# First batch of a fused attention and two-MLP kernel: kind of tile arithmetic and step counts set tile by tile, low parts on VectorE, the next batch's first loads on SP's queue

## The chip, the cores and the metric

The kernel runs on 1 core of one Trainium2 chip. The metric is the device time of one execution in microseconds; the number compared is a median over several executions. A core has TensorE (PE in the rows; its weight loads are PEld), VectorE (DVE), ScalarE (ACT), GpSimd (POOL) and SyncE (SP), which runs no arithmetic here and only issues transfers. Each engine works through its own instructions in the order in which they stand; between engines semaphores order the work. POOL and ACT can issue transfers too.

## The reference, cut to what matters

```python
def _attn_ref(q, k, v, p):                     # 8 batches, 8 heads, 576 rows, 64 columns; p has 32 rows
    scale = 1.0 / np.sqrt(q.shape[-1])
    def sm_attn(qq, kk, vv):
        s = scale * np.matmul(qq, kk.transpose(0, 1, 3, 2))
        s = s - np.max(s, axis=-1, keepdims=True)
        a = np.exp(s)
        a = a / (np.sum(a, axis=-1, keepdims=True) + 1e-09)
        return np.matmul(a, vv)
    p_packed = sm_attn(p, k, v)
    return sm_attn(q, p_packed, p_packed)
...
    x = attn_out.transpose(0, 2, 1, 3).reshape(4608, 512)
    h = x @ w_in;  g = h - np.tanh(h);  x = g @ w_out            # first MLP: 512 -> 2048 -> 512
    h = x @ w_in2; r = np.maximum(h, 0.0)
    return (s * (r * r) + b) @ w_out2                             # second MLP, same sizes
```

The weights of both MLPs come as 64-bit floats, everything else as 32-bit floats.

## The kernel before

**Precision.** TensorE multiplies in a 32-bit format of its own that holds fewer bits than the inputs. Each operand is therefore split into a high part (a rounded copy) and a low part (what the copy left over), and a product is three passes: high by low, high by high, low by high. `gh` and `gl`, `a2h` and `a2l`, and the two halves of each `wo` and `z` tile are such pairs.

**Converting the first MLP's weights.** `w_in1` is handled as four column chunks `w1[c]`, each in two halves (`w1_steps(c, i)`), and `w_out1` as sixteen row tiles (`wo1_steps(j)`). `to_f32` turns 64-bit words into 32-bit floats with one ACT instruction (the absolute value of the high word, L119) and four DVE instructions (L121, L123, L126, L129). A `wo` tile then gets its high part by an ACT cast (L138) and its low part by a subtraction (L140), which stands on GpSimd for tiles 2 to 11 and on VectorE for the others.

**Work per tile.** Batch 0 is 32 tiles in four parts: two halves of the rows by two halves of the 16 hidden tiles. I number them 0 to 31 in the order in which they run; in the names of the instructions `h_0_1_3` is batch 0, row half 1, hidden tile 3, which is tile 11 of this count. A tile is: `mm1` (six passes into one of two PSUM banks `h`, L464), tanh on ACT, the activation h - tanh(h) and its split, and then, two tiles later, `mm2` (twelve passes into the accumulators `acc`, L504). The activation comes in three kinds. Kind "v": DVE subtracts (L473), ACT rounds `gh`, DVE subtracts again for `gl` (L135). Kind "b": DVE subtracts inside the PSUM bank (L481), ACT reads `gh` from it, TensorE subtracts `gh` from the bank with a matrix `minus` (L487), ACT reads `gl` (L488). Kind "p": TensorE does the first subtraction too (L484). In kinds "b" and "p" the bank becomes free for the tile after next only when `gl` has been read.

**What sets the order.** While the tiles are written out, a generator `fill` is advanced by `next(fill)`; one step is about one instruction of the conversions, of the products `z` (`zp`, made of `w1[c]` and the packed attention, which replace attention and first weight by one matrix per batch) or of the next batch's attention. A second generator `more` converts the second MLP's weights. How many steps stand behind each tile is a table: `SLOTS` and `AFTER` before, per part, with `CATCH_UP` later. `in_turn` runs groups of generators one group after the other and may advance the next group's first step early. `until` forces steps where a tile needs their result. So the numbers decide where each instruction stands on each engine. The loads of batch 1 (`second_loads`: `load_p`, `load_k`, `load_v`, `load_q`) are steps of `fill` too; `load_k` and `load_q` are sixteen transfers each of 32 partitions by 9 by 32 floats.

Of the kernel before, what the change touches and what calls it, by code (L numbers as in the profile page):

```python
# [18 lines left out]
def pack_attention_two_mlps(ctx, tc, q, k, v, p, w_in1, w_out1, w_in2, w_out2, s_in, b_in, out):  # L19
# [16 lines left out]
    C = 9  # L36
# [16 lines left out]
    LAND = 14  # L53
    W_K, W_P, W_PK, W_PV, W_E, W_Q = 5, 1, 5, 1, 7, 5

    AFTER, SLOTS = (6, 5, 4, 1), (5, 3, 4, 1)
    HOW = "p" * 8, "b" * 8, "v" * 8, "v" * 8
    AHEAD, CATCH_UP, FIRST_W = 13, 4, (23, 24, 25, 26, 27, 40, 41, 42, 43, 44)
    EXP_LO, EXP_HI = 2.0 ** -15, 2.0 ** 16 * 1.875
    assert 2 * R == P and NB == 2 * C and 4 * M == P and 2 * D == P and H * D == DM  # L60

# [99 lines left out]
    def load_k(b, g):  # L161
        for hp in range(2):
            h0 = 4 * g + 2 * hp
            t = apool.tile([P, 2, C, 32], F32, tag="kr", name=f"k_{b}_{g}_{hp}", bufs=2)
            rows = k[b, h0:h0 + 2].rearrange("h (r a n) d -> a r h n d", a=2, n=C)
            for a in range(2):
                for u in range(2):
                    p0 = (2 * a + u) * 32
                    for e in range(2):
                        nc.gpsimd.dma_start(out=t[p0:p0 + 32, e], in_=rows[a][:, e, :, u * 32:u * 32 + 32])  # L170
            k_t[b, g, hp] = t

    def load_v(b, g):

        t = apool.tile([P, 4, CT * D], F32, tag="v", name=f"v_{b}_{g}", bufs=1)
        src = v[b, 4 * g:4 * g + 4].rearrange("h (r c) d -> r h (c d)", c=C)
        nc.gpsimd.dma_start(out=t[:R], in_=src[:, :, :CT * D])
        nc.gpsimd.dma_start(out=t[R:, :, :(C - CT) * D], in_=src[:, :, CT * D:])
        v_t[b, g] = t.rearrange("r h (c d) -> r h c d", c=CT)


# [49 lines left out]
    def load_q(b, hf):  # L231
        for g in range(G):
            for hp in range(2):
                h0 = 4 * g + 2 * hp
                t = apool.tile([P, HB // 32, 32], F32, tag="qr", name=f"q_{b}_{hf}_{g}_{hp}", bufs=4)
                for u in range(2):
                    for e in range(2):
                        src = q[b, h0 + e, hf * HB:(hf + 1) * HB, u * 32:u * 32 + 32]
                        p0 = (2 * e + u) * 32
                        nc.gpsimd.dma_start(out=t[p0:p0 + 32], in_=src.rearrange("(n r) d -> r n d", r=32))  # L240
                q_t[b, hf, g, hp] = t

    def bank_a(name):
# [312 lines left out]
    with tc.manual_schedule():  # L556
# [51 lines left out]
        def wo1_steps(j):  # L608
            while j == NF - 1 and ("wo", 13) not in done:
                yield  # L610
            src = stg["wo", j]
            x = words(src)[0].bitcast(F32)
            yield from to_f32(x, src, wopool.tile([P, 2, DM], I32, tag=f"wo{j}", name=f"t_{j}")[:, 0])
            yield from split_wo(j, "wo1", nc.gpsimd if 1 < j < 12 else nc.vector, x)
            done.add(("wo", j))
            if j in (5, 7):
                load_wo1(j + 3, j + 4)
            if j == 11:
                load_wo1(13)
            if j == NF - 1:  # L620
                free()
# [16 lines left out]

        def in_turn(*groups):

            groups = [[call_late(g) for g in group] for group in groups]
            for n, group in enumerate(groups):
                for i, _ in enumerate(both(group)):
                    yield
                    if i == min(AHEAD, 4 * len(group)) and n + 1 < len(groups):
                        for g in groups[n + 1]:
                            next(g)

        def call_late(f):
            g, *a = f  # L650
            yield from g(*a)

        def until(key, gen):
            forced.append(key)
# [16 lines left out]
        take_turn()  # L671
        load_wo1(0, 1, 2, 3, 4, 5, 6, 7)
        make_identity(nc, ident)
        nc.scalar.mul(minus, ident, -1.0)
        nc.vector.memset(ones, 1.0)

        run(step_p(0))
# [13 lines left out]
        def first_weights():  # L691
            yield from in_turn(
                [(w1_steps, 1, 0)], [(w1_steps, 1, 1)],
                [(wo1_steps, 0), (wo1_steps, 1)],
                [(first_z, 1), (wo1_steps, 2), (wo1_steps, 3)],
                [(wo1_steps, 4), (wo1_steps, 5)],
                [(second_stage, 0, 1), (wo1_steps, 6), (wo1_steps, 7)],
                [(w1_steps, 2, 0)], [(w1_steps, 2, 1)],
                [(wo1_steps, 8), (wo1_steps, 9)],
                [(first_z, 2), (wo1_steps, 10), (wo1_steps, 11)],  # L700
                [(w1_steps, 3, 0)], [(w1_steps, 3, 1)],
                [(wo1_steps, 12), (wo1_steps, 13), (second_loads,)],
                [(first_z, 3), (wo1_steps, 14), (wo1_steps, 15)])

        pend = []

# [103 lines left out]
        def slot():  # L810
            ticks[0] += 1
            if owed[0]:
                owed[0] -= 1
                next(fill, None)
            if ("wo", NF - 1) not in done:
                n = SLOTS[part[0]]
                for _ in range(ticks[0] * n // 6 - (ticks[0] - 1) * n // 6):
                    next(fill)
                return
            if ticks[0] % 3 == 1:  # L820
                next(more, None)
            next(fill, None)

        owed = [0]

        def owe():
# [4 lines left out]
        for b in range(B):  # L831
            if b:
                parts = [(hf, range(NF)) for hf in range(2)]
            else:
                parts = [(hf, js) for js in (range(NF // 2), range(NF // 2, NF)) for hf in range(2)]
            for hf, js in parts:
                part[0] += 1
                last = (b == B - 1 and hf == 1)
                if last:
                    until(("a", b, hf), fill)  # L840
                    run(fill)
                    run(more)
                    att.close()
                    second = SecondMLP(tc, ctx, wslot, w2_d, wo2_d, x2t, g2_d, s_sb, bias, out)
                    fill = second.early(lambda c: (B - 1, 1, c) in mm1_done)
                acc = new_acc(f"{b}_{hf}_{js[0]}")
                for j in js:
                    c = j // CH
                    until(("z", b, c), fill)
                    until(("a", b, hf), fill)  # L850
                    h = mm1(b, hf, j, slot)
                    if ("wo", NF - 1) not in done:
                        for _ in range(AFTER[part[0]]):
                            next(fill)
                    elif ("a", 1, 0) not in done:
                        for _ in range(CATCH_UP):
                            next(fill)
                    if j % CH == CH - 1:
                        mm1_done.add((b, hf, c))
                    how = HOW[part[0]][j - js[0]] if b == 0 else "v"  # L860
                    on_pe = how != "v"
                    t = act_bank(h, f"{b}_{hf}_{j}", how == "p") if on_pe else act1(h, f"{b}_{hf}_{j}")
                    if on_pe:
                        next(t)
                    between = None
                    if pend and len(pend[-1]) == 5:
# [471 lines left out]
```

## Time and profile before

| | |
|---|---|
| time, median of 3 executions | 1519.46 us (1517.79 to 1522.28) |
| the profiled execution's own time | 1515.79 us |
| its span, first to last instruction | 1514.0 us |
| TensorE busy over the span | 97% |
| VectorE, ScalarE, GpSimd busy over the span | 71%, 50%, 24% |
| mean granted TensorE clock | 0.990 of full speed |

The profiled execution is one of its own and lies below the three timed ones. Its time is 1.79 us more than its span. Busy shares are averages over the whole kernel; the change touches the first batch, which runs from about 36 to 172 us, and the loads of the second.

### The profile page before, as it was taken

How to read it: one execution, taken by the hardware profiler on the slowest of the kernel's cores; microseconds unless marked ns; L12 is line 12 of the kernel's file. 1: busy time of each engine (PE TensorE's matmuls, PEld its weight loads, DVE VectorE, ACT ScalarE, POOL GpSimd, SP SyncE). 2: the span in 40 equal slices, each digit the busy share in tenths (PEclk: the TensorE clock that was granted, in tenths of full speed). 3: DMA queues.
4: the chain of work that ended last, by engine and by line, in shares of the span. 5: the costliest groups of instructions: out<-in, count | busy, mean ns of one | idle time of the engine just before them, and what ended most of it. 6: DMA issues, size and time to landing. Idle time of an engine off the chain costs nothing.

```text
span 1514.0 us, 28111 instructions
## 1 busy us (share of the span) xinstructions
PE 1463.3 (97%) x10508; PEld 1377.0 (91%) x10508; DVE 1074.3 (71%) x2058; ACT 754.1 (50%) x1459; POOL 357.9 (24%) x576
## 2 busy tenths in 40 slices
PE   6779899999999999999999999999999999999998
PEld 4668798998988889889999999999999999999998
DVE  5886878879687887875555767767777775565564
ACT  4554344444444344443344556656667655454443
POOL 0248452634447274543001000000021000000000
PEclk7899999999999999999999999999999999999999
DMA  9446355544535354332428466465487987676683
GB/s 283 162 135 169 105 147 138 155 132 120 150 98 151 92 141 118 103 94 95 147 100 308 178 229 235 172 260 214 194 296 284 312 258 199 217 239 200 216 248 84
DMA packets 252185, 271.62 MB, mean 179 GB/s; under 512 B 112784, under 2 KB 191888, under 8 KB 252048
## 3 DMA queue, kind: packets, MB, share of 16 engines
q1 hardware_dynamic: 225952, 222.68, 44.9%
q0 software_dynamic: 22368, 46.17, 11.4%
q8 instruction: 82, 1.34, 0.4%
q10 hardware_dynamic: 3728, 0.98, 0.3%
q14 instruction: 55, 0.45, 0.1%
HBM read 161.61 MB, written 108.13 MB: 178 GB/s over the span
## 4 chain that ended last, share of the span: by engine, by line
PE 79%; issue 7%; DVE 6%; DMA 3%; POOL 3%; ACT 2%; SPq 1%; DVEq 0%; POOLq 0%; ACTq 0%
PE acc L504 22%; PE h L464 11%; PE Y L1271 9%; PE Y L1045 8%; PE Z L1271 6%; PE X L1045 6%; PE Z L1045 6%; PE X L1271 6%; PE zp L367 2%; POOL k L170 1%; DMA k<-in_k_dram 1%; DVE gl L135 1%; PE pv L339 1%; SPq L194 1%; DMA g<-g 1%
## 5 line engine op out<-in xcount | busy, mean ns | idle before, releaser
L504 PE MATMUL acc<-gh,wo 128*128 128x288 f32 x2040 | 418.6, 296 | 0.2 <-DVE wo L140 0.2
L504 PEld LDWEIGHTS acc<-gh,wo 128*128 128x128 f32 x2040 | 329.8, 189 | 0.5 <-DVE wo L140 0.4
L504 PE MATMUL acc<-gl,wo 128*128 128x288 f32 x1020 | 309.8, 304 | 5.7 <-ACT wo L138 2.8
L472 ACT ACTIVATE t<-h 128x288 f32<-128x288 f32 x240 | 98.8, 412 | 304.4 <-PE h L464 263.5
L504 PEld LDWEIGHTS acc<-gl,wo 128*128 128x128 f32 x1020 | 192.4, 189 | 34.7 <-issue 20.0
L464 PE MATMUL h<-a2h,z 128*128 128x288 f32 x1024 | 213.9, 297 | 1.5 <-ACT z L445 1.5
L473 DVE TENSOR_TENSOR t<-h,t 128x288 f32<-128x288 f32 x240 | 107.5, 448 | 139.5 <-ACT t L472 138.8
L944 DVE TENSOR_TENSOR x<-B,x 128x768 fp32r<-128x768 f32 x158 | 147.0, 950 | 74.3 <-ACT x L1201 60.4
L464 PE MATMUL h<-a2l,z 128*128 128x288 f32 x512 | 157.9, 308 | 9.8 <-ACT gl L488 6.4
L464 PEld LDWEIGHTS h<-a2h,z 128*128 128x128 f32 x1024 | 165.0, 189 | 2.2 <-ACT z L445 1.7
L240 POOL DMA_DIRECT2D q<-in_q_dram x224 | 135.3, 612 | 130.7 <-DVE qT L374 109.3
L1045 PE MATMUL Y<-x,w 128*128 128x384 f32 x864 | 158.5, 336 | 0.0
L1271 PE MATMUL Y<-x,w 128*128 128x384 f32 x864 | 153.4, 335 | 0.0
L1045 PEld LDWEIGHTS Y<-x,w 128*128 128x128 f32 x864 | 151.3, 188 | 0.0
L1271 PEld LDWEIGHTS Y<-x,w 128*128 128x128 f32 x864 | 150.2, 188 | 0.5 <-ACT x L1201 0.3
L170 POOL DMA_DIRECT2D k<-in_k_dram x224 | 136.6, 617 | 50.2 <-DVE kT L290 40.7
L464 PEld LDWEIGHTS h<-a2l,z 128*128 128x128 f32 x512 | 97.4, 190 | 27.1 <-ACT gl L488 9.4
L1201 ACT CAST x<-B 128x768 fp32r<-128x768 f32 x116 | 93.8, 834 | 42.6 <-DMA B<-g 30.2
L135 DVE TENSOR_TENSOR gl<-t,gh 128x288 fp32r<-128x288 f32 x239 | 110.8, 463 | 0.0
L1045 PE MATMUL X<-x,w 128*128 128x384 f32 x576 | 108.1, 336 | 0.0
L1045 PE MATMUL Z<-x,w 128*128 128x384 f32 x576 | 107.9, 336 | 0.0
L1271 PE MATMUL X<-x,w 128*128 128x384 f32 x576 | 103.0, 336 | 1.5 <-DVE w L944 1.5
(181 smaller groups left out, 2236.4 us busy)
## 6 DMA issues: line engine op xcount, KB each, us to landing
g<-g SPq DMA_DIRECT2D x190, 384.0 KB, 3.3
B<-g SPq DMA_DIRECT2D x116, 384.0 KB, 4.7
w<-w_d POOLq DMA_DIRECT2D x28, 512.0 KB, 6.1
B<-x2t SPq DMA_DIRECT2D x24, 384.0 KB, 5.4
g<-s SPq DMA_DIRECT2D x23, 384.0 KB, 2.8
out_dram<-g SPq DMA_DIRECT2D x184, 48.0 KB, 1.9
x2t<-xs SPq DMA_DIRECT2D x15, 576.0 KB, 3.7
w1s<-in_moe_w_in_dram SPq DMA_DIRECT2D x16, 512.0 KB, 8.1
```

The costliest lines, as they stand in the source:

```text
L135: (eng or nc.vector).tensor_tensor(out=lo, in0=x, in1=hi.bitcast(F32), op=ALU.subtract)
L170: nc.gpsimd.dma_start(out=t[p0:p0 + 32, e], in_=rows[a][:, e, :, u * 32:u * 32 + 32])
L240: nc.gpsimd.dma_start(out=t[p0:p0 + 32], in_=src.rearrange("(n r) d -> r n d", r=32))
L367: nc.tensor.matmul(ps[e][i * M:(i + 1) * M, :rhs(i).shape[-1]], pblk[b][r, h // 4, h % 4 * M:h % 4 * M + M], rhs(i)[r], start=True, stop=True)
L464: nc.tensor.matmul(h[:, :HB], zt[:, zi, g, f0:f0 + P], a[:, g], start=(n == 0), stop=(n == 3 * G - 1))
L472: nc.scalar.activation(t, h[:, :HB], AF.Tanh)
L473: nc.vector.tensor_tensor(out=t, in0=h[:, :HB], in1=t, op=ALU.subtract)
L504: nc.tensor.matmul(acc[m][:, :HB], w[:, m * P:(m + 1) * P], x, start=(j == js[0] and i == 0), stop=(j == js[-1] and i == 2))
L944: self.nc.vector.tensor_tensor(out=o, in0=a, in1=b, op=op)
L1045: self.nc.tensor.matmul(bank[:, f, :self.TH], w[:, f, a, kt], x[:, b, kt], start=(p in ("P1", "P5", "P6") and m == 0), stop=(m == 5), skip ...
L1201: self.nc.scalar.copy(self.xs[(7 * self.NBK + n) % self.XS][:, 0], self.ready[0])
L1271: nc.tensor.matmul(bank[:, ft, :T], w[:, kk, u, ft], x[:, v, kk], start=first and p in ("P1", "P5", "P6"), stop=last, skip_group_check=True)
```

## The change

Seven edits go together.

- The kind of each of batch 0's 32 tiles stands in one string `HOW`, and the number of `fill` steps per tile in one table `STEPS`. Before it was eight "p", eight "b", sixteen "v" (kinds per part). After it is sixteen "p", nine "b", seven "v". A tile's steps are spread over its six slots; the extra steps right behind `mm1` (`AFTER`, `CATCH_UP`) are gone.
- All low parts of `wo` are made by VectorE.
- `in_turn` advances the next group's first step (the absolute value on ACT) once each generator of the present group has run once, and only for weight conversions.
- Batch 1's K, V and Q are loaded by SP's queue instead of GpSimd's, and their step comes before the conversion of `w1[3]`.
- The conversion of `wo` tiles 12 and 13 stands beside `first_z(3)`, 14 and 15 after it.
- `more` starts, as before, when the last `wo` tile is done, but the slots of `fill` go on by the table until batch 1's first attention is done.
- `minus` is made by GpSimd from a zeroed tile instead of by ScalarE.

```diff
-    AFTER, SLOTS = (6, 5, 4, 1), (5, 3, 4, 1)
-    HOW = "p" * 8, "b" * 8, "v" * 8, "v" * 8
-    AHEAD, CATCH_UP, FIRST_W = 13, 4, (23, 24, 25, 26, 27, 40, 41, 42, 43, 44)
+    STEPS = 9, 13, 14, 11, 15, 10, 12, 15, 0, 6, 9, 13, 7, 5, 0, 2, 6, 3, 10, 5, 6, 10, 11, 11, 18, 14, 15, 13, 12, 13, 10, 8
+    HOW = "ppbbpppppppppvvvvvvpppvbbbbpbbbp"
+    FIRST = (0, 0, 8), (1, 0, 8), (0, 8, 16), (1, 8, 16)
...
-                        nc.gpsimd.dma_start(out=t[p0:p0 + 32, e], in_=rows[a][:, e, :, u * 32:u * 32 + 32])
+                        (nc.gpsimd if b > 1 else nc.sync).dma_start(out=t[p0:p0 + 32, e], in_=rows[a][:, e, :, u * 32:u * 32 + 32])
...
-            yield from split_wo(j, "wo1", nc.gpsimd if 1 < j < 12 else nc.vector, x)
+            yield from split_wo(j, "wo1", nc.vector, x)
...
-                    if i == min(AHEAD, 4 * len(group)) and n + 1 < len(groups):
-                        for g in groups[n + 1]:
-                            next(g)
+                    if i == len(group) and n + 1 < len(groups):
+                        for f, g in groups[n + 1]:
+                            if f in (w1_steps, wo1_steps):
+                                next(g)
...
-        nc.scalar.mul(minus, ident, -1.0)
+        nc.vector.memset(csum, 0.0)
+        nc.gpsimd.tensor_tensor(out=minus, in0=csum[:, 0], in1=ident, op=ALU.subtract)
...
+                [(second_loads,)],
                 [(w1_steps, 3, 0)], [(w1_steps, 3, 1)],
-                [(wo1_steps, 12), (wo1_steps, 13), (second_loads,)],
-                [(first_z, 3), (wo1_steps, 14), (wo1_steps, 15)])
+                [(first_z, 3), (wo1_steps, 12), (wo1_steps, 13)],
+                [(wo1_steps, 14), (wo1_steps, 15)])
...
-            if ("wo", NF - 1) not in done:
-                n = SLOTS[part[0]]
-                for _ in range(ticks[0] * n // 6 - (ticks[0] - 1) * n // 6):
+            if ("wo", NF - 1) in done and ticks[0] % 3 == 1:
+                next(more, None)
+            if ("a", 1, 0) in done or tile[0] >= len(STEPS):
+                next(fill, None)
+                return
+            n = STEPS[tile[0]]
+            for _ in range(ticks[0] * n // 6 - (ticks[0] - 1) * n // 6):
+                if ("a", 1, 0) not in done:
                     next(fill)
-                return
-            if ticks[0] % 3 == 1:
-                next(more, None)
-            next(fill, None)
...
-                    if ("wo", NF - 1) not in done:
-                        for _ in range(AFTER[part[0]]):
-                            next(fill)
-                    elif ("a", 1, 0) not in done:
-                        for _ in range(CATCH_UP):
-                            next(fill)
...
-                    how = HOW[part[0]][j - js[0]] if b == 0 else "v"
+                    how = HOW[tile[0]] if b == 0 else "v"
```

SP's order after the first store of partial sums, before the change. `wo1s_13` is the raw form of `wo` tile 13, `wo1s_7` that of tiles 14 and 15 together, `pc_1` batch 1's P, `xs` and `xp` the partial sums.

```order
L522 DMA x2t_138<-xs_0_0_906 512x1x288
L599 DMA wo1s_13_1033<-in_moe_w_out_dram 128x512
L229 DMA pc_1_1085<-in_p_dram 128x2x64 x2
L581 DMA wo1s_7_1088<-in_moe_w_out_dram 128x2x512
L522 DMA x2t_138<-xs_0_1_1273 512x1x288
```

The same place on SP after the change:

```order
L600 DMA wo1s_13_1038<-in_moe_w_out_dram 128x512
L230 DMA pc_1_1059<-in_p_dram 128x2x64 x2
L171 DMA k_1_0_0_1065<-in_k_dram 32x9x32 x8
L171 DMA k_1_0_1_1074<-in_k_dram 32x9x32 x8
L178 DMA v_1_0_1124<-in_v_dram 64x4x320
L179 DMA v_1_0_1124<-in_v_dram 64x4x256
L241 DMA q_1_0_0_0_1136<-in_q_dram 32x9x32 x4
L241 DMA q_1_0_0_1_1141<-in_q_dram 32x9x32 x4
L241 DMA q_1_0_1_0_1146<-in_q_dram 32x9x32 x4
L241 DMA q_1_0_1_1_1151<-in_q_dram 32x9x32 x4
L582 DMA wo1s_7_1228<-in_moe_w_out_dram 128x2x512
```

Thirty-four transfers of batch 1 now stand between the raw `wo` tile 13 and the raw tiles 14 and 15.

VectorE's order around the end of `wo` tiles 10 and 11 and the conversion of `w1[3]`, before the change (`t_10` is scratch; `h_0_1_3` and the like are the first subtraction of a tile of kind "b"):

```order
L481 TENSOR_TENSOR h_0_1_3_964<-h_0_1_3_964,t_0_1_3_976 128x288
L129 SCALAR_TENSOR_TENSOR wo1s_10_761<-wo1s_10_761,t_10_933 128x512
L129 SCALAR_TENSOR_TENSOR wo1s_11_763<-wo1s_11_763,t_11_935 128x512
L481 TENSOR_TENSOR h_0_1_4_998<-h_0_1_4_998,t_0_1_4_1013 128x288
L121 TENSOR_SCALAR w1_3_836<-w1_3_836 128x1024
L123 TENSOR_SCALAR w1_3_836<-w1_3_836 128x1024
L126 SCALAR_TENSOR_TENSOR w1_3_836<-w1s_3_0_837,w1_3_836 128x1024
L129 SCALAR_TENSOR_TENSOR w1_3_836<-w1s_3_0_837,w1_3_836 128x1024
```

The same place after the change:

```order
L141 TENSOR_TENSOR wo1_10_1010<-wo1s_10_758,wo1_10_1010 128x512
L141 TENSOR_TENSOR wo1_11_1012<-wo1s_11_760,wo1_11_1012 128x512
L474 TENSOR_TENSOR t_0_1_5_1043<-h_0_1_5_1034,t_0_1_5_1043 128x288
L474 TENSOR_TENSOR t_0_1_6_1090<-h_0_1_6_1083,t_0_1_6_1090 128x288
L136 TENSOR_TENSOR gl_1_0_1_6_1094<-t_0_1_5_1043,gh_1_0_1_6_1093 128x288
L474 TENSOR_TENSOR t_0_1_7_1116<-h_0_1_7_1109,t_0_1_7_1116 128x288
L136 TENSOR_TENSOR gl_1_0_1_7_1120<-t_0_1_6_1090,gh_1_0_1_7_1119 128x288
L122 TENSOR_SCALAR w1_3_862<-w1_3_862 128x1024
L474 TENSOR_TENSOR t_0_0_8_1171<-h_0_0_8_1163,t_0_0_8_1171 128x288
L136 TENSOR_TENSOR gl_1_0_0_8_1175<-t_0_1_7_1116,gh_1_0_0_8_1174 128x288
```

The two low parts have come onto VectorE, and the conversion of `w1[3]`, which stood behind tile 12's subtraction, now stands behind those of tiles 13 to 15.

ScalarE's order around the absolute value of `wo` tile 14 after the change (`z_0_3` is the product `z` of chunk 3):

```order
L473 ACTIVATE t_0_0_10_1258<-h_0_0_10_1249 128x288
L135 CAST gh_1_0_0_10_1261<-t_0_0_9_1203 128x288
L120 ACTIVATE t_14_1265<-wo1s_7_1228 128x512
L433 CAST z_0_3_1230<-zp_0_3_0_1231 128x512
L433 CAST z_0_3_1230<-zp_0_3_1_1232 128x512
L480 ACTIVATE t_0_0_11_1294<-h_0_0_11_1286 128x288
L135 CAST gh_1_0_0_11_1298<-t_0_0_10_1258 128x288
L139 CAST wo1_12_1308<-cv_139 128x512
L139 CAST wo1_13_1313<-wo1s_13_1038 128x512
L486 CAST gh_0_0_11_1295<-h_0_0_11_1286 128x288
L446 CAST z_0_3_1230<-zp_0_3_0_1231 128x512
L446 CAST z_0_3_1230<-zp_0_3_1_1232 128x512
```

The instruction that needs the raw tile 14 now stands ahead of all four casts of `z_0_3` and of tile 19's tanh; before, it stood after tile 15's tanh, and ahead of the same casts.

## Rows read from the trace of the kernel before

**Rows 1.** Three stretches: length; busy us (instructions) PE, PEld, DVE, ACT, POOL; PEclk; DMA share; GB/s.

```profile
35.70:74.61 38.91, 30.68 (x177) 24.23 (x178) 34.17 (x60) 23.33 (x49) 8.13 (x6) 0.87 0.47 175
74.61:111.38 36.77, 27.27 (x186) 21.82 (x186) 32.71 (x53) 21.04 (x47) 15.95 (x20) 0.95 0.47 141
...
122.77:171.62 48.85, 43.67 (x422) 33.53 (x420) 32.85 (x87) 18.54 (x55) 31.99 (x53) 1.00 0.59 143
```

**Rows 2.** TensorE's timeline: start, length, what, count, [idle before, and what ended it].

```profile
55.12 0.65 PE L484 MATMUL h<-t,minus 128*128 128x288 f32 x2
55.39 0.85 PE L442 MATMUL zp<-z,minus 128*128 128x512 f32 x2
...
74.61 0.40 PE L464 MATMUL h<-a2l,z 128*128 128x288 f32 x1 [0.23 <-DVE a2l L418]
...
96.94 0.40 PE L464 MATMUL h<-a2l,z 128*128 128x288 f32 x1 [1.08 <-ACT gl L488]
...
111.38 0.40 PE L464 MATMUL h<-a2l,z 128*128 128x288 f32 x1 [1.49 <-ACT gl L488]
...
122.77 0.29 PE L464 MATMUL h<-a2l,z 128*128 128x288 f32 x1
...
158.96 0.30 PE L464 MATMUL h<-a2l,z 128*128 128x288 f32 x1
...
161.37 0.29 PE L464 MATMUL h<-a2l,z 128*128 128x288 f32 x1
...
170.01 1.68 PE L367 MATMUL zp<-w,pblk 64*32 64x512 f32 x16 [2.48 <-DVE z L435]
171.62 0.40 PE L464 MATMUL h<-a2l,z 128*128 128x288 f32 x1
```

**Rows 3.** GpSimd's low parts: their group (busy us, mean ns), and the last two in time.

```profile
L140 POOL TENSOR_TENSOR wo<-wo1s,wo 128x512 fp32r<-128x512 f32 x10 | 13.8, 1391 | 83.8 <-ACT wo L138 83.8
...
95.82 3.04 POOL L140 TENSOR_TENSOR wo<-wo1s,wo 128x512 fp32r<-128x512 f32 x2 [4.97 <-ACT wo L138]
```

**Rows 4.** VectorE's timeline between 48 and 98 us.

```profile
48.24 1.29 DVE L140 TENSOR_TENSOR wo<-wo1s,wo 128x512 fp32r<-128x512 f32 x2
49.45 0.76 DVE L121 TENSOR_SCALAR t<-t 128x512 f32<-128x512 f32 x2
...
55.51 1.00 DVE L121 TENSOR_SCALAR t<-t 128x512 f32<-128x512 f32 x2 [2.23 <-ACT t L119]
56.43 1.85 DVE L123 TENSOR_SCALAR t<-t 128x512 int32<-128x512 int32 x2
...
75.56 0.69 DVE L121 TENSOR_SCALAR w<-w 128x1024 f32<-128x1024 f32 x1
...
83.50 0.76 DVE L121 TENSOR_SCALAR t<-t 128x512 f32<-128x512 f32 x2
...
89.81 0.47 DVE L481 TENSOR_TENSOR h<-h,t 128x288 f32<-128x288 f32 x1 [1.38 <-ACT t L479]
...
93.63 1.28 DVE L129 SCALAR_TENSOR_TENSOR wo1s<-wo1s,t 128x512 int32<-128x512 int32 x2
...
97.73 1.69 DVE L123 TENSOR_SCALAR w<-w 128x1024 int32<-128x1024 int32 x1
```

**Rows 5.** SP's timeline, two issues; then SP's output stores from 1495 us (ns min/median/max).

```profile
17.51 5.29 SPq L194 DMA_DIRECT2D rows<-in_q_dram  x6
...
100.32 0.42 SPq L581 DMA_DIRECT2D wo1s<-in_moe_w_out_dram  x1
...
L1233 SPq DMA_DIRECT2D out_dram<-g x16: 315/414/472, 1497.9 to 1510.8; - x16
```

**Rows 6.** Issues of 98.8 to 119 us, median us to landing; an ACT group (busy, mean ns).

```profile
wo1s<-in_moe_w_out_dram SPq DMA_DIRECT2D x1, 1024.0 KB, 8.3
k<-in_k_dram POOLq DMA_DIRECT2D x16, 36.0 KB, 4.6
...
L119 ACT ACTIVATE t<-wo1s 128x512 f32<-128x512 f32 x15 | 9.5, 675 | 0.0
```

More of the change, by code (lines that the diff above doesn't have):

```diff
@@ L54, in pack_attention_two_mlps @@
     W_K, W_P, W_PK, W_PV, W_E, W_Q = 5, 1, 5, 1, 7, 5
-    AFTER, SLOTS = (6, 5, 4, 1), (5, 3, 4, 1)
-    HOW = "p" * 8, "b" * 8, "v" * 8, "v" * 8
-    AHEAD, CATCH_UP, FIRST_W = 13, 4, (23, 24, 25, 26, 27, 40, 41, 42, 43, 44)
+    STEPS = 9, 13, 14, 11, 15, 10, 12, 15, 0, 6, 9, 13, 7, 5, 0, 2, 6, 3, 10, 5, 6, 10, 11, 11, 18, 14, 15, 13, 12, 13, 10, 8
+    HOW = "ppbbpppppppppvvvvvvpppvbbbbpbbbp"
+    FIRST = (0, 0, 8), (1, 0, 8), (0, 8, 16), (1, 8, 16)
+    FIRST_W = 23, 24, 25, 26, 27, 40, 41, 42, 43, 44
     EXP_LO, EXP_HI = 2.0 ** -15, 2.0 ** 16 * 1.875
@@ L176, in load_v @@
         src = v[b, 4 * g:4 * g + 4].rearrange("h (r c) d -> r h (c d)", c=C)
-        nc.gpsimd.dma_start(out=t[:R], in_=src[:, :, :CT * D])
-        nc.gpsimd.dma_start(out=t[R:, :, :(C - CT) * D], in_=src[:, :, CT * D:])
+        (nc.gpsimd if b > 1 else nc.sync).dma_start(out=t[:R], in_=src[:, :, :CT * D])
+        (nc.gpsimd if b > 1 else nc.sync).dma_start(out=t[R:, :, :(C - CT) * D], in_=src[:, :, CT * D:])
         v_t[b, g] = t.rearrange("r h (c d) -> r h c d", c=CT)
@@ L239, in load_q @@
                         p0 = (2 * e + u) * 32
-                        nc.gpsimd.dma_start(out=t[p0:p0 + 32], in_=src.rearrange("(n r) d -> r n d", r=32))
+                        (nc.gpsimd if b > 1 else nc.sync).dma_start(out=t[p0:p0 + 32], in_=src.rearrange("(n r) d -> r n d", r=32))
                 q_t[b, hf, g, hp] = t
@@ L639, in in_turn @@
         def in_turn(*groups):
-            groups = [[call_late(g) for g in group] for group in groups]
+            groups = [[(f, f(*a)) for f, *a in group] for group in groups]
             for n, group in enumerate(groups):
-                for i, _ in enumerate(both(group)):
+                for i, _ in enumerate(both([g for _, g in group])):
                     yield
-                    if i == min(AHEAD, 4 * len(group)) and n + 1 < len(groups):
-                        for g in groups[n + 1]:
-                            next(g)
-        def call_late(f):
-            g, *a = f
-            yield from g(*a)
+                    if i == len(group) and n + 1 < len(groups):
+                        for f, g in groups[n + 1]:
+                            if f in (w1_steps, wo1_steps):
+                                next(g)
         def until(key, gen):
@@ L814, in slot @@
                 next(fill, None)
-            if ("wo", NF - 1) not in done:
-                n = SLOTS[part[0]]
-                for _ in range(ticks[0] * n // 6 - (ticks[0] - 1) * n // 6):
+            if ("wo", NF - 1) in done and ticks[0] % 3 == 1:
[6 more added lines that the diff above has]
+                if ("a", 1, 0) not in done:
                     next(fill)
-                return
-            if ticks[0] % 3 == 1:
-                next(more, None)
-            next(fill, None)
+        tile = [-1]
         owed = [0]
@@ L834, in pack_attention_two_mlps @@
             else:
-                parts = [(hf, js) for js in (range(NF // 2), range(NF // 2, NF)) for hf in range(2)]
+                parts = [(hf, range(j0, j1)) for hf, j0, j1 in FIRST]
             for hf, js in parts:
@@ L848, in pack_attention_two_mlps @@
                     c = j // CH
+                    tile[0] += 1
                     until(("z", b, c), fill)
```

## The prediction

> **What bounds the kernel now.** I read the busy shares first. TensorE is busy 97% of the span (the table of the time before), so what can be won is its idle time, and that lies in batch 0: from 35.70 to 171.62 us it starts 32 tiles in 135.9 us. A tile without extras takes 161.37 - 158.96 = 2.41 us [rows 2]. From batch 1 on TensorE is practically never idle, so what batch 0 ends earlier the kernel ends earlier. The second MLP's conversion, which starts later after the change, I cost at nothing: TensorE's products of batches 1 and 2 hide it, and the second MLP's first product comes well after it; without that cover it would cost what it is late, at most the stretch by which it starts later.
>
> Then I cut batch 0 into stretches [rows 1]. From 35.70 to 74.61 us VectorE works 34.17 of 38.91 us and TensorE 30.68; from 74.61 to 111.38 VectorE 32.71 of 36.77, TensorE 27.27. Up to tile 16 VectorE is the bound. From 122.77 to 171.62 TensorE is busy 43.67 of 48.85 and leaves 5.2 us. Tiles 8, 13, 16 and 20 start at 74.61, 96.94, 111.38 and 122.77, batch 1's first at 171.62 [rows 2]; I follow the change from one of these to the next.
>
> **Tiles 0 to 8.** The change puts ten low parts on VectorE. A pair costs it 1.29 us, so five pairs cost 6.45; GpSimd needed 13.8 us for them, 1391 ns each [rows 3, 4]. But VectorE was held up while GpSimd subtracted: a pair of L121 took 1.00 instead of 0.76, of L123 1.85 instead of 0.76, a single L123 1.69 instead of 0.69 [rows 4]. I found eight such rows between the one at 55.51 and the one at 97.73, 6.0 us longer in all. So the move itself costs VectorE about nothing. The Trainium skill, page "SBUF — State Buffer", section "Who interferes with whom", says that VectorE and GpSimd share a port pair under an exclusive lock and that the loser waits fully; the trace shows 6.0 us of GpSimd's 13.8, and by a full block 13.8 would come back.
>
> Before tile 8 the sum is: three pairs added, 3.87 us; two tiles become "b", with a subtraction of 0.47 each, 0.94; given back 4.48 (six of the eight rows lie here), and the wait of 2.23 for the absolute value, which now runs a group ahead [rows 4]. Net -1.9: tile 8 at 72.7. `minus` on GpSimd costs nothing: GpSimd stands idle then, and the matrix is first read long after.
>
> **Tiles 8 to 16.** From 75.56 to 94.91 us (93.63 + 1.28) VectorE converts `w1[2]` and `wo` tiles 8 to 11 [rows 4]. Tiles 8 to 12 turn to "p": four subtractions of 0.47 fall away, and the wait of 1.38 for one of their tanhs; 0.53 is given back; the pair for tiles 8 and 9 adds 1.29. That is -2.5, with the -1.9 from before -4.4: the conversion of tiles 10 and 11 ends at 90.5, their low parts at 91.8, against 98.86 on GpSimd (95.82 + 3.04) [rows 3]. Tile 13 waited for `gl`, which stood on ScalarE behind casts of tiles 10 and 11 [rows 2]; it starts at 92.5. Tiles 13 to 15 are kind "v" now and need three times 2.41 and some passes of `z_2`, 0.5: tile 16 at 100.2 against 111.38.
>
> **The conversion of `w1[3]`.** It started at about 97 us; now it stands behind tile 15's subtraction on VectorE. Tile 15 starts at 97.8; with 1.5 for its product and 0.9 for tanh and subtraction the conversion starts at 100.2. It takes 83.50 - 75.56 = 7.94 less a subtraction of 0.47 [rows 4], 7.5, and between its steps stand two subtractions each for two "v" tiles, 1.9: ready at 109.6. The product with `w1[3]` stands on TensorE ahead of tile 18's first pass, so tile 18 starts at 110.7 with its 1.1 us. Tiles 16 and 17 end at 105, so here TensorE waits some 4 us: half of the 11 us is lost again.
>
> **SP's queue.** After the store of the raw `wo` tile 13's transfer comes batch 1's P, then 34 transfers of K, V and Q, then the raw tiles 14 and 15. The wait that SP stands in ends with tile 11's low part, 91.8 instead of 98.86; the two transfers ahead took until 100.32, 1.46 us [rows 5]; so the 34 begin at 93.3. What SP needs for one transfer with runs of 128 bytes from DRAM, the trace does not show. The nearest row is the output's stores, with runs of that length, 414 ns; the farthest the six large loads of Q, 5.29 / 6 = 882 ns, and below 0.41 I see no reason [rows 5]. I take 0.41, by the run length: 13.9 us, raw tiles 14 and 15 issued at 107.2 instead of 100.32. The same 1 MB landed 8.3 us after its issue, K's transfers 4.6 us [rows 6]. I take 6.2, since less else is moving then: landed at 113.4. The Trainium skill, page "DMA: Bandwidth & Descriptors", section "Queues, rings and completion order", says that what one engine issues is taken in ring order; by that the raw tiles' data also waits for the 34 loads' packets, which would take the 8.3; tile 20 would then come 2.1 us later than I say below.
>
> ScalarE comes to the absolute value of tile 14 at about 112.5 and waits 0.9 us. Behind it on ScalarE stand tile 18's `gh`, four casts of `z_3`, tile 19's tanh and casts of tiles 12 and 13: ten instructions, none above the 0.675 us of the absolute value [rows 6], by their sizes 4.8 us together. TensorE needs `z_3`'s low part for tile 20: 118.2 instead of 122.77, 4.6 earlier.
>
> **Tile 20 to batch 1**, 48.85 us before. Added on TensorE: four "p" tiles with three short passes, 55.39 - 55.12 = 0.27 for two [rows 2], so 0.40 each; seven "b" tiles with one, 0.13 each; 0.2 for a transposition: 2.7 us. Removed: the wait of 2.48 before batch 1's last `zp` and that product's 1.68, of which 1.1 returns a tile later [rows 2]; about 1.0 of waits for VectorE, which no longer converts the second MLP here (4.3 us). Sum: 2.7 - 2.48 - 0.58 - 1.0 = -1.4.
>
> **Sum.** -4.6 - 1.4 = -6.0 us against the profiled execution: span 1508.0, own time 1509.8. The median of the timed runs lies 3.67 above the profiled one's time, so the time to name is **1513.5 us**.
>
> **Rivals.**
> A, the forecast: gain 4.6 to 9, time 1510.5 to 1514.9. Chance 0.42.
> B, more is won: the raw tiles land before ScalarE asks for them and `w1[3]` is ready when tile 18 comes. Then tile 18 stands behind 16 and 17 with no wait, 105 + 1.1, and tile 20 at 106.1 + 4.8 = 110.9, with some 1 us of waits 112; gain 10.8 + 1.4 = 12.2, about 1507. For it speaks that VectorE's conversion may give back more than 6.0 of GpSimd's 13.8; against it, that the conversion is bound to tile 15 by its order. 9 us and more: 0.20. By the page's full block above, up to 7.8 us more would come back, and this would be the case.
> C, the gain is lost in the tail: batch 1's first attention fills the slots behind tile 20, and if its K arrives no earlier than before, or VectorE and ScalarE have more to do there per tile ("p" and "b" put two reads of the bank on ScalarE), tile 20's 4.6 are waited away and only part of the -1.4 is left: about 1518. Speaks for it: 5.2 us of idle in that stretch [rows 1] show that it is not TensorE's alone. Into it falls that the edits don't do what they say, for instance that VectorE's lengthened rows remain. Gain 0 to 4.6: 0.26.
> D, slower: SP needs 0.88 us for each of the 34 transfers. Then 93.3 + 29.9 + 6.2 + 4.8 = 134.2 for tile 20, 11.4 later than before, less 1.4: 10.0 slower, 1529.5. It decides from 0.58 us on: 34 times 0.17 us eat the 4.6 and the 1.4. For it speaks that these transfers read DRAM in 288 short runs like Q's larger ones; against it that the stores with such runs took 0.41. Chance 0.12.
>
> **Range and chances.** One execution of this kernel differs from another by about 0.3%, 4.6 us; less I call no change. A and B are faster: 0.62; C 0.26 within; D 0.12. The range takes A and nearly all of B and C: from 1505 (all of B's 12.2 and 2 us of its bound) to 1520.5 (C with a late attention of 1 us).
>
> **What the profile after would show.** On VectorE pairs of L121 and L123 at 0.76 with none lengthened; tile 11's low part ended near 92; tile 16 near 100; then a wait of TensorE of about 4 us before `zp` of chunk 3, released by VectorE; SP's loads of K and Q spaced by 0.41 us; a short wait of ScalarE for the raw tile 14; tile 20 at 118, batch 1 at 166 to 167. Wrong would make it: a spacing above 0.58 us; a tile 16 that stays near 107 because ScalarE's casts, not VectorE, release it; or idle TensorE behind tile 24 that waits for batch 1's attention.

## The result

The change made the kernel slower: 1526.54 us median of 8 executions (1524.5 to 1530.02) against 1518.33 of the kernel before, ratio 1.0055, interval 1.0044 to 1.0067. Forecast were 1513.5 us and a gain of 6.0.

The profiled execution has a span of 1525.8 us, 11.8 more than before; the medians differ by 8.2, since the profiled execution of the kernel before lies 2.5 us below its median and that of the changed kernel 1.1 above. The windows of batch 0, cut at tiles 8, 16, 20 and batch 1's first tile, answer to [rows 1]:

```profile
35.52:71.86 36.34, 29.57 (x173) 23.49 (x174) 34.55 (x69) 23.52 (x50) 0.00 (x0) 0.86 0.53 202
71.86:97.89 26.03, 24.61 (x181) 22.39 (x179) 20.57 (x36) 16.85 (x38) 0.00 (x0) 1.00 0.44 136
97.89:121.17 23.28, 16.05 (x95) 12.80 (x93) 15.06 (x26) 8.55 (x19) 0.00 (x0) 0.85 0.65 135
121.17:166.82 45.65, 44.28 (x427) 37.11 (x425) 31.69 (x81) 24.87 (x71) 11.10 (x18) 0.97 0.57 130
```

Up to tile 16 the change does what was forecast and more: tile 16 starts at 97.89 instead of 111.38. Then it gives the lead back: from tile 16 to 20 it takes 23.28 us instead of 11.39. TensorE's timeline shows where; it answers to [rows 2]:

```profile
97.89 0.29 PE L465 MATMUL h<-a2l,z 128*128 128x288 f32 x1
...
107.78 1.93 PE L368 MATMUL zp<-w,pblk 64*32 64x512 f32 x8 [3.30 <-DVE w L130]
109.64 0.61 PE L465 MATMUL h<-a2l,z 128*128 128x288 f32 x1
...
114.08 0.29 PE L465 MATMUL h<-a2l,z 128*128 128x288 f32 x1
...
119.97 0.75 PE L485 MATMUL h<-t,minus 128*128 128x288 f32 x2 [3.35 <-ACT t L480]
...
121.17 0.44 PE L465 MATMUL h<-a2l,z 128*128 128x288 f32 x1
...
166.82 0.51 PE L465 MATMUL h<-a2l,z 128*128 128x288 f32 x1
```

The lead is 13.5 us at tile 16, 6.8 at tile 18 (109.64 against 116.43), 1.6 at tile 20, 4.8 at batch 1's first tile. Part of the last is only order: before, a product of 1.68 us and the wait of 2.48 stood ahead of that tile, and the product now comes behind it. The two waits are the forecast ones, for `w1[3]` and, by way of ScalarE, for the raw tiles 14 and 15. SP's timeline, which answers to [rows 5], and ScalarE's:

```profile
92.25 8.20 SPq L171 DMA_DIRECT2D k<-in_k_dram  x16
...
101.89 9.50 SPq L241 DMA_DIRECT2D q<-in_q_dram  x16
111.49 0.40 SPq L582 DMA_DIRECT2D wo1s<-in_moe_w_out_dram  x1
```

```profile
117.98 0.66 ACT L120 ACTIVATE t<-wo1s 128x512 f32<-128x512 f32 x1 [5.77 <-DMA wo1s<-in_moe_w_out_dram]
```

That is not yet a loss. The transposition of P comes once per batch (`ppT`, start and length), and its last three show how the kernels stand to each other; first before, then after:

```profile
459.70 0.38 PE L254 MATMUL ppT<-ident,pc 128*128 128x128 f32 x2
552.83 0.38 PE L254 MATMUL ppT<-ident,pc 128*128 128x128 f32 x2
645.32 0.38 PE L254 MATMUL ppT<-ident,pc 128*128 128x128 f32 x2
```

```profile
458.27 0.38 PE L255 MATMUL ppT<-ident,pc 128*128 128x128 f32 x2
554.81 0.38 PE L255 MATMUL ppT<-ident,pc 128*128 128x128 f32 x2
653.31 0.38 PE L255 MATMUL ppT<-ident,pc 128*128 128x128 f32 x2
```

At 458 us the changed kernel is still ahead, by 1.4 us. At 553 it is 2.0 behind, at 645 8.0, and from about 700 us to the end some 11 to 12. So the time is lost between 460 and 700 us, in batches 4 to 6, far behind everything that the change moves by hand. The windows from the first tile of batch 4 to the first of batch 7, before and after:

```profile
443.76:722.61 278.85, 273.35 (x2404) 246.75 (x2403) 216.25 (x567) 117.14 (x327) 142.48 (x229) 1.00 0.41 113
```

```profile
442.63:734.10 291.47, 279.91 (x2404) 251.99 (x2403) 212.51 (x569) 118.46 (x329) 142.11 (x229) 0.98 0.42 113
```

The stretch takes 12.6 us more. TensorE stands idle 6.1 us longer in it (11.6 against 5.5), and for the same number of products it is busy 6.6 us longer, at a mean granted clock of 0.98 instead of 1.00. What runs there and not earlier is the second half of the second MLP's conversion. For each unit of `w_out2` GpSimd adds the converted rows into `csum` (L744), and VectorE may overwrite the converted tile (L752) only when that sum is made. The view of `csum`, before and after (instructions with ns min/median/max, then who waited for it, us and times):

```profile
L744 POOL TENSOR_TENSOR csum<-csum,cv x32: 729/742/848, 448.9 to 678.1; 128x256 f32<-128x256 f32 x32
...
  DVE cv L752: 5.5, 1
```

```profile
L744 POOL TENSOR_TENSOR csum<-csum,cv x32: 726/742/842, 458.5 to 701.4; 128x256 f32<-128x256 f32 x32
...
  DVE cv L752: 20.8, 4
...
  PE cs L768: 4.5, 1
```

One wait of VectorE has become four. The one before, on VectorE's timeline:

```profile
474.23 0.29 DVE L752 TENSOR_TENSOR cv<-cv 128x128 f32<-128x128 f32 x1 [5.51 <-POOL csum L744]
```

After the change, GpSimd's timeline at the third of the four, then VectorE's and TensorE's:

```profile
565.90 8.41 POOL L171 DMA_DIRECT2D k<-in_k_dram  x14 [0.25 <-DMA q<-in_q_dram]
574.33 1.64 POOL L744 TENSOR_TENSOR csum<-csum,cv 128x256 f32<-128x256 f32 x2
```

```profile
575.10 0.29 DVE L752 TENSOR_TENSOR cv<-cv 128x128 f32<-128x128 f32 x1 [5.48 <-POOL csum L744]
575.31 0.45 DVE L474 TENSOR_TENSOR t<-h,t 128x288 f32<-128x288 f32 x1
```

```profile
576.03 1.01 PE L768 MATMUL cs<-ones,csum 128*128 128x2 f32 x4 [4.54 <-POOL csum L744]
```

The sum takes 0.8 us, but it stands on GpSimd behind the issues of sixteen loads of Q and sixteen of K, 0.61 us each. VectorE waits for it with all that is behind it, the subtractions of the running tile first, and TensorE runs dry. From 568 to 582 us TensorE is busy 9.46 of 14 us, and its granted clock, 0.76 of 2.4 GHz on the mean, was not the full one throughout.

So I had three theories for the loss. **P**: the phase. The change starts the second conversion some tiles later, and in the program's order its sums now fall three times directly behind the 32 loads of Q and K on GpSimd, before only once. **R**: batch 0 leaves the later attention in another place, and the waits for `csum` are only where that shows. **T**: the second conversion is late as a whole.

### The profile page after: what moved, and what is told of

It reads as the page before. It is cut to its first block, busy times and chain, and to the rows that moved or that the text cites. A ratio compares the mean times of both kernels' runs of the same rounds, so it can differ in the third digit from the quotient of the medians.

```text
span 1525.8 us, 28157 instructions
## 1 busy us (share of the span) xinstructions
PE 1476.0 (97%) x10533; PEld 1389.0 (91%) x10533; DVE 1062.3 (70%) x2052; ACT 759.0 (50%) x1467; POOL 302.6 (20%) x499
## 3 DMA queue, kind: packets, MB, share of 16 engines
q0 software_dynamic: 20000, 42.63, 10.5%
## 5 line engine op out<-in xcount | busy, mean ns | idle before, releaser
L505 PEld LDWEIGHTS acc<-gh,wo 128*128 128x128 f32 x2040 | 333.5, 191 | 0.5 <-DVE wo L141 0.4
L473 ACT ACTIVATE t<-h 128x288 f32<-128x288 f32 x231 | 95.1, 412 | 309.8 <-PE h L465 268.8
L474 DVE TENSOR_TENSOR t<-h,t 128x288 f32<-128x288 f32 x231 | 103.6, 448 | 143.0 <-ACT t L473 141.7
L171 POOL DMA_DIRECT2D k<-in_k_dram x192 | 116.4, 614 | 188.5 <-DMA k<-in_k_dram 139.1
L241 POOL DMA_DIRECT2D q<-in_q_dram x192 | 115.9, 612 | 121.9 <-DVE qT L375 106.5
L136 DVE TENSOR_TENSOR gl<-t,gh 128x288 fp32r<-128x288 f32 x230 | 104.6, 455 | 4.4 <-ACT gh L135 4.4
```

Source lines behind the costliest of these rows:

```text
L136: (eng or nc.vector).tensor_tensor(out=lo, in0=x, in1=hi.bitcast(F32), op=ALU.subtract)
L171: (nc.gpsimd if b > 1 else nc.sync).dma_start(out=t[p0:p0 + 32, e], in_=rows[a][:, e, :, u * 32:u * 32 + 32])
L241: (nc.gpsimd if b > 1 else nc.sync).dma_start(out=t[p0:p0 + 32], in_=src.rearrange("(n r) d -> r n d", r=32))
L473: nc.scalar.activation(t, h[:, :HB], AF.Tanh)
L474: nc.vector.tensor_tensor(out=t, in0=h[:, :HB], in1=t, op=ALU.subtract)
L505: nc.tensor.matmul(acc[m][:, :HB], w[:, m * P:(m + 1) * P], x, start=(j == js[0] and i == 0), stop=(j == js[-1] and i == 2))
```

## The experiments

Ratios are to the kernel before, run on the same chip, with their 95% intervals. The changed kernel stands at 1.0055.

**e1**, in the kernel before:

```diff
-            yield from wait(LAND)
+            yield from wait(LAND + 7)
```

> The kernel before; only the second MLP's conversion starts 7 of its steps later, so that on GpSimd its sums of the second output weight stand among the loads of K and Q just as in the changed kernel. Batch 0 is untouched. Theory P (the phase of that conversion against GpSimd's loads is what costs): VectorE waits four times instead of once for a sum that stands behind some 10 us of loads, TensorE runs dry and its clock falls, and the time is 6 to 13 us above the kernel before, 1524 to 1531. Rival R (the loss comes from how batch 0 and the first attention leave the later batches, not from the second conversion): no change, 1518 within 3 us. Rival T (the second conversion is late as a whole, its last products are waited for): a wait of TensorE near 730 us, about 9 us more.

Measured: 1526.8 us, ratio 1.0052 (1.0038 to 1.0066), all of the change's net loss with none of its edits. The view of `csum`:

```profile
  DVE cv L752: 17.4, 4
  PE cs L768: 6.0, 1
```

I had expected batch 0 to be untouched, and it was not: with the conversion out of its end TensorE is quicker there (the account of tile 20 to batch 1 below has the numbers), so batches 4 to 6 lose that lead as well as the 0.5%.

**e2**, the other way round in the changed kernel (`LAND - 7`).

> The changed kernel; only the second MLP's conversion starts 7 of its steps earlier, which puts its sums among GpSimd's loads nearly as in the kernel before (one run of 32 loads with a sum behind it instead of three). Theory P: 6 to 12 us below the changed kernel, 1515 to 1520, with at most two of VectorE's waits of 5 us for a sum left. Rival R: no change, 1526 within 3 us. Rival T: 9 us less too, but without the waits for a sum being what went.

Measured: 1516.27 us, ratio 0.9976 (0.9965 to 0.9988), 0.8% or 12 us below the changed kernel. One wait is left:

```profile
  DVE cv L752: 3.5, 1
```

**e3** in the changed kernel, **e4** in the kernel before:

```diff
-                        nc.gpsimd.memset(csum, 0.0)
+                        nc.vector.memset(csum, 0.0)
...
-                        nc.gpsimd.tensor_tensor(out=csum, in0=csum, in1=xa[:, 2 * kh:2 * kh + 2], op=ALU.add)
+                        nc.vector.tensor_tensor(out=csum, in0=csum, in1=xa[:, 2 * kh:2 * kh + 2], op=ALU.add)
```

> The changed kernel; the sums of the second output weight's rows are added by VectorE itself, 32 instructions of some 0.45 us, 14 us of its time in all, instead of by GpSimd, where they stood behind the loads. Theory P: the four waits of 5 us are gone, 8 to 13 us less than the changed kernel, 1513.5 to 1518.5. Rival R: nothing gained, or 1 to 3 us lost by VectorE's extra work, 1526 to 1529.

> The control: the kernel before with the same edit of the sums. It has one wait of 5.5 us for a sum, at 474 us, behind which TensorE stood idle 1.4 and 1.2 us. Theory P: 1 to 3 us less than before, 1515 to 1517.5. If the sums cost in general and not by their phase (rival R), it gains as much as the changed kernel does by the edit.

Measured: e3 1511.64 us, ratio 0.9951 (0.9938 to 0.9964); e4 1514.77 us, ratio 0.9965 (0.9953 to 0.9978). The edit is worth 1.04% or 15.8 us in the changed kernel and 0.35% or 5.3 us in the kernel before. The difference, 10.5 us, is what the phase cost. That e4 gained more than the 1 to 3 us expected is a miss. Its trace lacks the wait at 474 us, and from the first tile of batch 4 to the first of batch 5, where that wait stood, its lead grows by 2.7 us (0.9 to 3.6) and hardly changes after that; where the rest of the 5.3 comes from stays open.

**e12**, e4 with e1's delay.

> The control of e1 and e4 together: the kernel before with the sums on VectorE (e4, ratio 0.9965) and with the second MLP's conversion 7 steps later (e1, ratio 1.0052 with the sums on GpSimd). Theory P (only the sums' place among GpSimd's loads makes the start of that conversion matter): as e4, 0.9965, at most 0.002 away. Rival T (its later start costs by itself) or any other effect of the delay: 0.87 per cent above e4 as in e1, 1.003 to 1.006.

Measured: 1511.32 us, ratio 0.9943 (0.9922 to 0.9963). The delay that cost 0.5% with the sums on GpSimd costs nothing with them on VectorE. The stretch from the first tile of batch 4 to the first of batch 7 says the same in the traces: 278.85 us before, 291.47 in the changed kernel, 292.23 in e1, but 275.76 in e2, 275.90 in e3, 276.31 in e4 and 275.99 in e12. P stands; R and T fall.

What is left is batch 0: e3 against e4 and e12, 0.9951 against 0.9965 and 0.9943, puts the whole change without the phase between 2 us of gain and 1 us of loss, where 6.0 of gain were forecast. The next kernels start from e3 and change batch 1's loads, the steps of tiles 14 to 17, or both; only e11 starts from e4. The edits of the change were not all tried one by one: the kinds in `HOW`, the step table as a whole, `in_turn`, the place of `wo` tiles 12 to 15 and `minus` never were.

**e5**: Q's loads behind the raw tiles.

```diff
-                [(second_loads,)],
+                [(second_loads, load_p, load_k, load_v)],
...
-                [(first_z, 3), (wo1_steps, 12), (wo1_steps, 13)],
+                [(second_loads, load_q), (first_z, 3), (wo1_steps, 12), (wo1_steps, 13)],
```

> All four kernels of this set are e3 (the changed kernel with the sums on VectorE, so that no phase of the second conversion disturbs) with one edit. Here the sixteen loads of batch 1's Q come behind the load of the raw tiles 14 and 15 on SP's queue. Theory Q (batch 0 gave only 2 us because SP's 34 loads make those raw tiles late): they are issued near 103.5 us instead of 111.5, ScalarE's wait of 5.8 us for them, TensorE's of 3.35 and the fall of its clock at 120 us are gone, tile 20 comes at 116 to 118 instead of 121.2, and the time is 3.5 to 5 us below e3, ratio to before 0.992. Rival K (tile 20's start doesn't matter, since the first attention of batch 1 sets the end of batch 0): within 1 us of e3, 0.995.

Measured: 1505.59 us, ratio 0.9915 (0.9899 to 0.9932), 5.5 us below e3. SP's and TensorE's timelines:

```profile
102.92 0.55 SPq L582 DMA_DIRECT2D wo1s<-in_moe_w_out_dram  x1
103.52 11.88 SPq L241 DMA_DIRECT2D q<-in_q_dram  x16
```

```profile
108.38 1.06 PE L368 MATMUL zp<-w,pblk 64*32 64x512 f32 x8 [3.30 <-DVE w L130]
```

The raw load goes out at 102.9, ScalarE's long wait for it is gone, tile 20 starts 79.0 us after tile 0 (e3: 85.8). The wait for `w1[3]` is as long as in e3.

**e6** (steps of tiles 14 to 17) and **e7** (e5 and e6 together):

```diff
-    STEPS = 9, 13, 14, 11, 15, 10, 12, 15, 0, 6, 9, 13, 7, 5, 0, 2, 6, 3, 10, ...
+    STEPS = 9, 13, 14, 11, 15, 10, 12, 15, 0, 6, 9, 13, 7, 5, 5, 6, 0, 0, 10, ...
```

> e3 with eleven steps moved: tiles 14 to 17 advance 5, 6, 0, 0 steps instead of 0, 2, 6, 3, so that VectorE converts w1[3] from about 94 us on. TensorE's wait of 3.3 us before its product and the half clock from 108 to 114 us go, tile 18 starts at 103 to 105 instead of 109.6. Theory Q: the raw tiles 14 and 15 still land near 118, tile 20 stays within 1.5 us of 121, and the time within 1.5 us of e3, 0.994 to 0.995: the two delays lie one behind the other and the later one decides. Rival C (TensorE's wait and its clock are what cost): 5 us less, 0.992.

> e3 with both edits, those of e5 and e6. Theory Q: raw tiles issued at 102 and landed by 109, w1[3] ready by 103, tile 20 at 110 to 113 instead of 121.2, 8 to 11 us below e3, ratio to before 0.988 to 0.990, more than e5 and e6 together. Rival K: within 2 us of e3.

Measured: e6 1510.15 us, ratio 0.9946 (0.9929 to 0.9962), within what was expected; e7 1507.84 us, ratio 0.9925 (0.9909 to 0.9941), a miss. Neither tells anything on theory Q, since the edit missed its aim: eleven steps by the end of tile 15 also carried the product with `w1[3]` ahead of tile 16 on TensorE, and the wait of 3.4 us stood there (e6: 102.51 us) instead of ahead of tile 18. Hence:

**e9**, e5 with steps 5, 5, 0, 1.

> e5 (sums on VectorE, Q's loads behind the raw tiles 14 and 15) with steps moved so that VectorE converts w1[3] from about 95 us on and the product that needs it keeps its place behind tile 17: tiles 14 to 17 advance 5, 5, 0, 1 steps instead of 0, 2, 6, 3. In e6 and e7 eleven steps by tile 15 had carried that product ahead of tile 16 on TensorE, and the wait of 3.3 us stood there instead. Theory Q: the wait and the half clock behind it go, tile 18 starts 67 to 69 us after tile 0 instead of 73.2 in e5; the raw tiles still land near 110 us, so that tile 20 gains less than tile 18 does: 79.0 less 1 to 3 us, and the time is 1 to 3 us below e5, ratio to before 0.9895 to 0.991. Rival K (tile 20 is not what counts): as e5, 0.9915.

Measured: 1503.18 us, ratio 0.9895 (0.9882 to 0.9909), the lowest of all, though its interval overlaps e5's. On TensorE's timeline the wait is 1.87 us, for a tile's `gl` behind the conversion on VectorE, and the product waits for nothing:

```profile
101.19 0.40 PE L505 MATMUL acc<-gl,wo 128*128 128x288 f32 x1 [1.87 <-DVE gl L136]
...
103.78 1.60 PE L368 MATMUL zp<-w,pblk 64*32 64x512 f32 x16
```

Tile 18 starts 71.1 us after tile 0, later than the 67 to 69 expected, tile 20 78.0 us, one less than in e5. Of the 2.8 us between the two profiled executions 0.7 lies between tile 0 and the last tile of batch 7 (749.95 against 750.63 us) and 1.8 in the second MLP's products, which the edit doesn't touch. So only some 1 us is shown to be the edit's.

**e10**: all of batch 1's loads behind the raw tiles.

```diff
-    STEPS = 9, 13, 14, 11, 15, 10, 12, 15, 0, 6, 9, 13, 7, 5, 0, 2, 6, 3, 10, ...
+    STEPS = 9, 13, 14, 11, 15, 10, 12, 15, 0, 6, 9, 13, 7, 5, 2, 3, 0, 6, 10, ...
...
-                [(second_loads,)],
...
-                [(first_z, 3), (wo1_steps, 12), (wo1_steps, 13)],
+                [(second_loads,), (first_z, 3), (wo1_steps, 12), (wo1_steps, 13)],
```

> e3 with all 34 loads and P behind the load of the raw tiles 14 and 15, and w1[3] converted early with its product behind tile 17 (tiles 14 to 17 advance 2, 3, 0, 6 steps). Theory Q: raw tiles issued about 100 us, landed by 107, tile 20 at 74 to 77 us after tile 0 instead of 85.8 in e3, and if batch 1's K, loaded from 101 to 110 us, is still in time, 9 to 11 us below e3, ratio 0.988 to 0.990. Rival K: K comes too late now, TensorE waits for batch 1's first scores near 125 to 130 us, and the gain is that of e5 at most, 0.9915 or above.

Measured: 1507.02 us, ratio 0.992 (0.9907 to 0.9934): rival K. The raw tiles go out at 91.63 us, earlier than the 100 expected, and tile 20 comes earliest of all, 76.1 us after tile 0, but the second group of K's loads starts at 125.53 us on SP instead of 122.88 (e5), and VectorE waits for it:

```profile
135.49 0.84 DVE L291 STREAM_TRANSPOSE kT<-k 128x288 f32<-128x288 f32 x2 [3.59 <-DMA k<-in_k_dram]
```

TensorE waits 3.39 us for the scores behind it, until 136 us, later than the 125 to 130 expected. Which of the loads on SP goes first is a trade between these two waits.

**e8**: batch 1's loads by GpSimd again (`b > 0` for `b > 1` in the four places of the diff).

> e3 with batch 1's K, V and Q issued by GpSimd again, which has nothing else to do in batch 0 now. Raw tiles 14 and 15 wait only for their buffer and are issued near 103.5. Theory Q: 3.5 to 5 us below e3 like e5, 0.992, if GpSimd's 34 issues of 0.61 us, from about 92 to 113 us, bring K in time. Rival K, or GpSimd too slow: TensorE waits for the first scores of batch 1 near 130 us, and it is even with e3 or 1 to 3 us slower.

Measured: 1510.58 us, ratio 0.9947 (0.9932 to 0.9962), even with e3, though tile 20 comes 81.8 us after tile 0 instead of 85.8. Most of the 4 us is lost before tile 0, which starts at 39.07 instead of 35.91; in all other runs but e11 it starts between 34.27 and 36.22. GpSimd's timeline at the start of e8, and SP's in e8 and in e3:

```profile
1.40 0.45 POOL L673 TENSOR_TENSOR minus<-csum,ident 128x128 fp32r<-128x128 f32 x1
1.89 9.24 POOL L171 DMA_DIRECT2D k<-in_k_dram  x15
```

```profile
8.54 12.29 SPq L195 DMA_DIRECT2D v<-in_v_dram  x5
```

```profile
8.45 9.05 SPq L195 DMA_DIRECT2D v<-in_v_dram  x5
```

In the kernel before, GpSimd's low parts stood ahead of these loads and held them back. With the low parts gone it issues batch 1's K at 1.9 us, into batch 0's own loads, and SP needs 12.29 us instead of 9.05 for those of V.

**e11**, in e4:

```diff
-            yield from split_wo(j, "wo1", nc.gpsimd if 1 < j < 12 else nc.vector, x)
+            yield from split_wo(j, "wo1", nc.vector, x)
```

> e4 (the kernel before with the sums on VectorE) with all low parts of wo made by VectorE and nothing else of the change. My count in the prediction: VectorE gets 6.45 us more work and 6.0 us back from rows that GpSimd lengthened, so the lengthened rows are gone and tile 16 moves by less than 2 us; with tile 12's wait for the last low parts shorter the time is 0 to 3 us below e4, ratio 0.9945 to 0.9965. Rival: VectorE is the bound up to tile 16 and pays for the work, tile 16 is 4 to 6 us later and the time 3 to 6 us above e4, 0.998 to 1.0005.

Measured: 1516.92 us, ratio 0.9989 (0.9979 to 0.9998), 3.6 us above e4, as the rival said, but not by its mechanism: from tile 0 to tile 16 it takes 76.0 us, e4 75.8. The loss lies ahead of tile 0, which starts 3.6 us later than in e4, with GpSimd's K loads at 1.5 us and SP's V loads taking 12.24 us (9.53 in e4).

## Why the prediction was wrong, by its steps

**The second MLP's conversion, "which starts later after the change, I cost at nothing".** This step failed. I looked only at whether it is done in time, and it is. But it doesn't lie under batches 1 and 2, as I wrote: its sums run from 448.9 to 678.1 us before, in batches 4 to 6. What its start also sets is where its sums fall among GpSimd's loads, which recur in every batch. e1 makes the loss by that alone, e2 takes it back, e3 and e4 put the phase's cost at 10.5 us, and e12 shows that with the sums elsewhere a later start costs nothing. The trace of before had the mechanism in a row: the wait of VectorE of 5.51 us at 474 us. With it fell the step "what batch 0 ends earlier the kernel ends earlier": of the 2.4 us won by the fifth tile of batch 1 nothing is left after batch 4. No rival named the phase; my slower case was SP's queue.

**Tiles 0 to 16** were right in kind and a little small: tile 8 at 71.86 (72.7 forecast), tile 16 at 97.89 (100.2). No pair of L122 or L124 (L121 and L123 before) is lengthened now; the pairs at 49.89 and 55.64 us take 0.75 and 0.76 as forecast [rows 4]. VectorE's work from tile 0 to 8 is 34.55 us against 34.17 [rows 1], with three pairs more in it. e11 confirms that moving the low parts costs VectorE nothing net: from tile 0 to tile 16 it is busy 67.02 us, in e4 66.84. One of the eight rows was misread: the pair at 55.51 us was over at 56.51, before GpSimd's first subtraction at 56.69, and its 0.24 us were a short idle gap; that is small against the 6.0. The Trainium skill, page "SBUF — State Buffer", section "Who interferes with whom", has the loser of the shared port wait fully. That by this all 13.8 us of GpSimd's subtractions would come back to VectorE was my reading, not the page's, which names only some of VectorE's instructions as contending; VectorE would then be busy some 7 us less in e11 than in e4, and it is not.

**`w1[3]`**: right in kind. Waits of 0.58 and 3.30 us, some 4 forecast, tile 18 at 109.64 (110.7).

**SP's queue**: the term that was mis-sized in batch 0. K's transfers took 8.20 / 16 = 0.51 us each and Q's 0.59, where I took 0.41 from the last sixteen of the output's stores; the 34 took 0.57 on the mean ((111.49 - 92.25) / 34). The page of before had these very transfers at 0.61 on GpSimd, a nearer row. The raw tiles went out at 111.49 instead of 107.2. Their landing in 6.5 us (6.2 forecast) was right. Tile 20 came at 121.17 instead of 118.2, so 1.6 us earlier than before and not 4.6. e5 takes that delay away: tile 20 comes 6.8 us earlier than in e3, counted from tile 0, and the time is 5.5 us less. That is more than the 3.0 us by which tile 20 came too late, since TensorE's clock stayed up there too (see below). The middle of my own bounds, 0.41 to 0.88, would have been nearer.

**Tile 20 to batch 1**: forecast a gain of 1.4; by the fifth tile of batch 1 the lead is 2.4 us (179.82 against 182.23), so 0.8 came. Inside it the term for VectorE, "about 1.0 of waits" saved because the second MLP's conversion is gone from here, was too small. e1 and e12 have that later start alone, and from tile 20 to the fifth tile of batch 1 they take 55.71 and 55.56 us, against 59.46 before and 59.14 in e4: 3.6 to 3.8 us. So the other edits together cost about 3 us in this stretch; which of them, no run shows.

**In sum**: -6.0 were forecast and +8.2 measured, a miss of 14.2 us. The phase makes 10.5 of it. Batch 0, which gave about 2 instead of 6.0, makes the rest.

## What to carry to other kernels

When a change moves the start of background work that recurs with its own period, don't ask only whether it ends in time: look for what it shares an in-order engine with, and count how often a short instruction that others wait for falls behind a long run of issues. Here the engine that issues transfers one by one was a poor place for arithmetic on which another engine waits; moving it took that dependence on the start away. And work that is taken off an engine may have been what held back the transfers behind it: ask what that engine issues first now.

## What was not expected of the hardware

TensorE's granted clock after the same wait was not the same. In the changed kernel and e3, 103 to 114 us, with the wait of 3.30 us for `w1[3]`, it was 0.69 and 0.70, and tile 18 to tile 19 took 4.44 us; in e5, with a wait of 3.30 us for the same product, it stayed at 1.00 and that took 2.52 us. The windows of the changed kernel and of e5:

```profile
103.00:114.00 11.00, 7.28 (x34) 4.74 (x35) 8.13 (x17) 1.46 (x5) 0.00 (x0) 0.69 0.71 114
```

```profile
103.00:114.00 11.00, 7.55 (x57) 5.60 (x56) 9.75 (x18) 4.06 (x11) 0.00 (x0) 1.00 0.81 188
```

What made the difference these runs don't settle. Of e5's 5.5 us some part, 1.9 us between tiles 18 and 19 alone, is therefore the clock's and not SP's.

Loads of one engine slow those of another at the start of the kernel: with sixteen of K by GpSimd beside them, SP's five loads of V took 12.2 to 12.3 us in e8 and e11 and 9.05 in e3. The Trainium skill, page "DMA: Bandwidth & Descriptors", section "Issuing engines are not separate DMA queues", says that transfers of all engines run on the same sixteen DMA engines and interleave there. The longer V loads agree with that; no run here shows where they waited.
